# An attention block with a GLU block: VectorE's share of the exponentials as four bit patterns, and projections as column tiles

## The chip, the cores and the metric

The kernel runs on one core of a Trainium2 chip. The metric is device time in microseconds. A profile of one execution stands beside it, with the start and length of the instructions on each engine: TensorE (PE; its weight loads are PEld), VectorE (DVE), ScalarE (ACT), GpSimd (POOL) and SyncE (SP), which issues the DMAs.

## The reference

One transformer layer on 2048 rows of 640 bf16 numbers. There are 32 heads of 20 numbers, so 2048 x 2048 scores for each head.

```python
qkv = (layernorm(x) @ wqkv).reshape(1, 2048, 3, 32, 20)     # q, k, v
scores = einsum("bhqd,bhkd->bhqk", q, k) * 20 ** -0.5
p = softmax(scores, axis=-1)
h = x + einsum("bhqk,bhkd->bhqd", p, v).reshape(1, 2048, 640) @ wo
n = layernorm(h)
out = h + (gelu(n @ w_gate) * (n @ w_up)) @ w_down          # inner width 1728
```

## The kernel before

**Tiles, units and slots.** Scores are computed with the keys on the partitions: a tile is 128 keys by 512 columns in one PSUM bank, made by `qk_mms` (L873) from 32-row tiles of the array, one head in each row group, so that up to four matmuls run at once. The queries are cut into seven chunks, c0 to c6, of 512, 512, 256, 256, 256, 128 and 128 rows (`SIZES`). A chunk is worked through in slots: a slot holds 512 columns of queries and heads (one group of four heads for 512 queries, two groups for 256, four for 128) against all keys, which is always 64 tiles. There are 32 slots (8, 8, 4, 4, 4, 2, 2) and 2048 tiles. A quad is the four tiles of one group of heads and one stretch of keys, one for each head `j`.

ScalarE takes the tiles in units of two or three neighbouring banks, with one `exp` ACTIVATE for each unit (`unit`). In c0 and c4 to c6 the units use banks 0 to 2 and 3 to 4 in turn; in c1 to c3 banks 0 to 2 and 3 to 5 (`PAT`). The results lie in a ring of 18 tiles (`PR` in pts, `PR2` in pts2, which the profile names rege).

**VectorE's exponentials.** Some tiles are left to VectorE (`D_PER_SLOT`: 8 a slot, 2 in the first slot, 6 in c6; 246 in all). `d_exp` reads the scores out of PSUM as 16-bit integers of the exponent scaled by 512 (L831). For each pair of such tiles six operations follow on 1024 columns: two make the mantissa, two square and multiply, one adds, and one turns the sum into the bit pattern of a bf16 number. A VectorE tile's scores go to a spare bank (`BG`), or in c1 to c3 into the third bank of a unit.

**Value matmuls.** Exponentials of a tile are multiplied with 21 columns of `v_all` (20 values and a one, for the softmax's sum) in column tiles of the array, `tile_position=(0, 32 * j)`, so that the four heads of a quad run at once and add up in bank 6 for the whole slot. Two quads go together (`PV_QUADS`). VectorE's tiles are added to quads of ScalarE's that lack a head, at least eight units later (`D_LAG`), and the rest at the slot's end. At the end of a slot `epilogue` copies bank 6 out, transposes it (fp32, L984) and divides by the sums.

**Work around it.** Before the first exponential come layer norm, transposes of x (L576), and the first projections. The other projections of q, k and v run during c0 (`chain`, L631, full 128 x 128 array; evictions on VectorE at L661 and L764). After each chunk `post` makes wo (also `chain`), the second layer norm, gate and up matmuls (`mms`, L1061), GELU on ScalarE in blocks of up to 2048 columns, the product (L1107), the down matmul (L1118) and the output, while the next chunks' exponentials run. What c6 needs, and what c5 left over, comes at the end.

**The order of the work.** The program is a list of operations with reads, writes and PSUM banks. `Sched.schedule` plans it: each engine takes the ready operation of best priority (scores and exp 0, value matmuls 1, projections 1.5 to 3, GLU 3) by costs written into the code, and the planned order is fixed for each engine. Each TensorE operation has a mode: "row" for scores, "col" for value matmuls, "full" for the rest. A change of mode is costed at 0.098 us, and behind an operation of one mode a ready one of the same mode is preferred. `due` is the time by which the next score group must start; an operation that would run past it is passed over. Where TensorE would be idle, the planner adds matmuls that keep its clock up: pads on bank 6 (zero weights, column tiles) and `warm` matmuls on bank 7.

Of the kernel before, what the change touches and what calls it, by code (L numbers as in the profile page):

```python
# [7 lines left out]
ALU = mybir.AluOpType  # L8
# [35 lines left out]
class Sched:  # L44
# [46 lines left out]
    def schedule(self):  # L91
# [23 lines left out]
        while done < total:  # L115
# [4 lines left out]
            for e in ENGINES:  # L120
# [8 lines left out]
                while ready[e]:  # L129
# [203 lines left out]
def bass_sequential_preLN__mha_block__glu_gated_geglu__prompt_kernel(  # L333
# [12 lines left out]
    with ExitStack() as es:  # L346
# [48 lines left out]
        E_WORDS = 19200  # L395
# [39 lines left out]
        dv = [ka[:, 1024 * i:1024 * i + 1024].bitcast(I16) for i in range(ND - 2)]  # L435
        pts2 = carve(PR2 * 512)


        carve = carver(qt_all[:, 0, :, :].rearrange("p g s -> p (g s)"), NG * 512)
        dv += [carve(1024).bitcast(I16) for _ in range(2)]  # L440
        df1 = carve(1024)
        dw1 = carve(1024).bitcast(F16)
        dv0 = [ha_f[:, 1024 * i:1024 * i + 1024].bitcast(I16) for i in range(ND)]
        df0, dw0 = ha_f[:, 1024 * ND:1024 * ND + 1024], ha_f[:, 1024 * ND + 1024:1024 * ND + 2048].bitcast(F16)
# [184 lines left out]
        def chain(bk, key, n, steps, reads, prio, acq=True, after=()):  # L629
            for k, (l, r) in enumerate(steps):  # L630
                yield op("pe", lambda eng, l=l, r=r, k=k: eng.matmul(  # L631
                    bank(bk, n), l, r, start=(k == 0), stop=(k == len(steps) - 1)),
                    c_mm(n), prio, mode="full", util=n / 2400.0, reads=reads, writes=[key], acq=[bk] if (k == 0 and acq) else [],
                    after=after if k == 0 else ())

# [145 lines left out]
        PAT = [((0, 1, 2), (3, 4, 5)) if c in (1,2,3) else ((0, 1, 2), (3, 4)) for c in range(len(CHUNKS))]  # L781
        units, ubank, dtile, ends = [], [], [], []
        i, in_slot = 0, {}
        while i < len(tiles):
            s_ = tiles[i][0]
            c = slots[s_][0]
            bs = PAT[c][len(units) % 2]
            k = in_slot.setdefault(s_, [0, 0])
            nd = D_PER_SLOT[c] if s_ else D_SLOT0
            units.append(tiles[i:i + len(bs)])  # L790
            ubank.append(bs[0])
            six = len(PAT[c][1]) == 3
            i += len(units[-1])
            want = min(nd, (k[0] - D_FIRST) * nd // D_SPAN + 1) if k[0] >= D_FIRST else 0
            if six and k[1] < want and len(units[-1]) == 3 and units[-1][2][0] == s_:
                dtile.append(units[-1].pop())
                k[1] += 1
            elif not six and k[1] < want and tiles[i][0] == s_:
                dtile.append(tiles[i])
                k[1] += 1  # L800
                i += 1
            else:
                dtile.append(None)
            k[0] += 1
            ends.append(i)
        assert all(k[1] % 2 == 0 for k in in_slot.values())
        d_tiles = set(x for x in dtile if x)
        x_unit = {}
        for u, tl in enumerate(units):
            for x in tl + [dtile[u]]:  # L810
                x_unit[x] = u
        pv_bank = {}
        pv_open = set()
        pv_wait = []
        last_qk = {c: [] for c in range(len(CHUNKS))}
        d_raw, d_done = [], []
        d_n = [0]
        d_ops = []
# [3 lines left out]
        def d_exp(b, tile, prio):  # L822

            i, h = (d_n[0] // 2) % ND, d_n[0] % 2
            d_n[0] += 1
            assert all(x[1] != ("dv", i) for x in d_done)
            early = slots[tile[0]][0] == 0
            v = (dv0 if early else dv)[i]
            df, dw = (df0, dw0) if early else (df1, dw1)
            aft = tuple(e_ops) if early else tuple(e_ops) + tuple(last_qk[0])  # L830
            d_ops.append(op("dve", lambda eng: eng.tensor_scalar(v[:, 512 * h:512 * h + 512], bank(b), EXP_MUL, -32000.0,  # L831
                                                                 ALU.mult, ALU.max), c_dve(512), P_QK,
                            reads=[("SD", tile)], writes=[("dv", i)], rel=[b], after=aft))
            d_raw.append(tile)
            if h == 0:
                return
            zi = df.bitcast(I16)
            d = lambda fn, n, r, w: d_ops.append(op("dve", fn, 0.066 + n, prio, reads=r, writes=w))
# [6 lines left out]
            for k, tl in enumerate(d_raw):  # L845
                d_done.append((v[:, 512 * k:512 * k + 512].bitcast(BF16), ("dv", i), tl))
            d_raw.clear()

        def unit(u):
# [56 lines left out]
            while pv_wait:  # L906

                quads = []
                while pv_wait and len(quads) < PV_QUADS:
                    x0 = pv_wait[0][2]  # L910
                    have = [x for x in pv_wait if x[2][:3] == x0[:3]]
                    want = 4 - sum(1 for j in range(4) if x0[:3] + (j,) in d_tiles)
                    if len(have) < want or quads and quads[0][0][2][0] != x0[0]:
                        break
                    del pv_wait[0:want]
                    quads.append(have)
                if not quads:
                    return
                s_ = quads[0][0][2][0]
                c, gs = slots[s_]  # L920
                q0, nq = CHUNKS[c]
                nk = 512 // nq
                final = quads[-1][0][2][1:3] == (gs[-1], NT // nk - 1)
                if len(quads) < PV_QUADS and not final:
                    pv_wait[0:0] = [x for h in quads for x in h]
                    return

                for have in quads:
                    for x in list(d_done):
                        if u - x_unit[x[2]] >= D_LAG and x[2][3] not in [y[2][3] for y in have]:  # L930
                            have.append(x)
                            d_done.remove(x)
                while final and d_done:
                    have = []
# [276 lines left out]
```

## Time and profile before

| what | value |
|---|---|
| runs of the kernel, us | 923.36, 927.22, 928.9 (median 927.22) |
| the profiled execution: span, us | 923.6 |
| ScalarE busy, us (share) | 887.4 (96%), 786 instructions |
| TensorE busy, us (share) | 835.0 (90%), 10070 matmuls |
| VectorE busy, us (share) | 760.3 (82%), 1562 instructions |
| exp ACTIVATEs: of three tiles, of two | 394, 310 |
| first exp starts, last ends, us | 35.3, 891.3 |
| granted TensorE clock, mean | 0.996 |

The profiled execution's own time is known as its span, 923.6 us, which lies at the lower end of the three runs. "Busy" is the time in which at least one instruction of the engine runs. A matmul of 512 columns is shown with 0.38 us, though one can start every 0.217 us; so TensorE's busy share says little of how full it is, and the prediction counts array time instead. Consecutive exps overlap in the same way by about 0.2 us. A group's line in the profile gives: line, engine, operation, out<-in, partitions x elements and type, count | busy us, mean ns of one | idle time of the engine just before them, and what ended it.

### The profile page before, as it was taken

What the parts mean: (1) busy time and instruction counts of PE and PEld (TensorE: products, weight loads), DVE (VectorE), ACT (ScalarE), POOL (GpSimd) and SP (SyncE); (2) the same over time, 40 slices, a digit from 0 to 9 for tenths busy, and PEclk for the clock granted to TensorE, in tenths of its full rate; (3) what the DMA queues carried; (4) which work ended last, traced back from release to release, by engine and by line L of the source; (5) the groups of instructions that cost most, each with busy time, mean ns of one, the idle gap of its engine ahead of it and who ended that gap; (6) DMA issues with size and microseconds to landing.
All of it is one profiled execution on the core that took longest, in us unless ns stands there. A gap on an engine that the chain in (4) does not pass through costs nothing.

```text
span 923.6 us, 23026 instructions
## 1 busy us (share of the span) xinstructions
PE 835.0 (90%) x10070; PEld 353.3 (38%) x10070; DVE 760.3 (82%) x1562; ACT 887.4 (96%) x786; POOL 34.4 (4%) x117
## 2 busy tenths in 40 slices
PE   3999999999998997999788997889999999998998
PEld 2432232222222222233233332334445455565666
DVE  8859999899897896888698995878898769997653
ACT  7899999999999999999999999999999999999981
POOL 5000000000001000000001000000101000001000
PEclk9999999999999999999999999999999999999999
DMA  7301021222721000000111000000100000110000
GB/s 258 95 21 41 17 55 48 71 56 67 228 99 30 1 2 1 1 8 16 37 30 30 2 2 1 2 23 24 44 17 16 1 9 23 26 37 10 10 16 16
DMA packets 39516, 34.36 MB, mean 37 GB/s; under 512 B 19436, under 2 KB 36936, under 8 KB 39416
## 3 DMA queue, kind: packets, MB, share of 16 engines
q1 hardware_dynamic: 39416, 32.89, 12.6%
q8 instruction: 79, 1.29, 0.6%
q14 instruction: 21, 0.17, 0.1%
HBM read 20.12 MB, written 8.09 MB: 31 GB/s over the span
## 4 chain that ended last, share of the span: by engine, by line
ACT 73%; PE 20%; DVE 4%; DMA 2%; SPq 0%; issue 0%
ACT pts L354 46%; ACT rege L354 26%; PE ps L873 5%; PE ps L1061 5%; PE ps L354 4%; PE ps L631 3%; PE ps L1118 3%; DMA regw<-in_A_wqkv_dram 1%; DVE rege L354 1%; ACT L354 1%; DVE rege L831 1%; DVE qt_all L354 1%; PE ps L576 0%; DMA rege<-o_nat 0%; DVE rege L1107 0%; SPq L354 0%
## 5 line engine op out<-in xcount | busy, mean ns | idle before, releaser
L354 ACT ACTIVATE pts<-ps 128x1536 bf16<-128x1536 f32 (+1 forms) x474 | 573.2, 1378 | 5.6 <-PE ps L873 4.5
L873 PE MATMUL ps<-qt_all,kt_all 32*128 32x256 bf16 (+2 forms) x3584 | 289.6, 289 | 48.9 <-ACT pts L354 28.3
L354 ACT ACTIVATE rege<-ps 128x1536 bf16<-128x1536 f32 (+1 forms) x230 | 292.1, 1380 | 2.1 <-PE ps L873 1.1
L873 PEld LDWEIGHTS ps<-qt_all,kt_all 32*128 32x128 bf16 x3584 | 91.3, 92 | 271.5 <-ACT pts L354 155.9
L1061 PE MATMUL ps<-rege,regw 128*128 128x256 bf16 (+2 forms) x980 | 159.2, 292 | 10.5 <-DVE rege L1107 4.8
L354 DVE TENSOR_TENSOR qt_all<-qt_all 128x1024 f16<-128x1024 f16 (+1 forms) x235 | 160.6, 683 | 3.3
L831 DVE TENSOR_SCALAR rege<-ps 128x512 int16<-128x512 f32 x152 | 104.3, 686 | 39.7 <-PE ps L873 38.8
L354 PE MATMUL ps<-pts,v_all 128*21 128x256 bf16 (+2 forms) x2122 | 136.3, 290 | 0.0
L354 PE MATMUL ps<-rege,v_all 128*21 128x256 bf16 (+2 forms) x1278 | 108.2, 292 | 0.0
L1061 PEld LDWEIGHTS ps<-rege,regw 128*128 128x128 bf16 x980 | 73.3, 98 | 70.9 <-issue 24.1
L631 PE MATMUL ps<-regw 128*128 128x512 bf16 (+1 forms) x360 | 87.0, 350 | 2.9 <-DVE v_all L764 1.4
L1118 PE MATMUL ps<-regw,rege 128*128 128x320 bf16 x448 | 78.3, 301 | 2.6 <-DVE rege L1107 1.6
L354 DVE TENSOR_SCALAR qt_all<-qt_all 128x1024 int16<-128x1024 int16 (+1 forms) x188 | 75.9, 420 | 1.5
L831 DVE TENSOR_SCALAR qt_all<-ps 128x512 int16<-128x512 f32 x94 | 64.3, 684 | 3.3 <-PE ps L873 3.0
L354 DVE TENSOR_TENSOR rege<-rege 128x1024 f16<-128x1024 f16 (+4 forms) x103 | 65.4, 644 | 0.8
L354 PEld LDWEIGHTS ps<-pts,v_all 128*21 128x21 bf16 x2122 | 49.2, 91 | 38.2 <-issue 32.6
L354 DVE TENSOR_SCALAR rege<-rege 128x1024 int16<-128x1024 int16 (+2 forms) x136 | 55.4, 424 | 1.2
L354 PE MATMUL ps<-kt_all,zer 128*32 128x512 bf16 x608 | 51.9, 385 | 0.0
L1107 DVE TENSOR_TENSOR rege<-rege,ps 128x512 bf16<-128x512 bf16 (+1 forms) x53 | 35.8, 678 | 19.3 <-PE ps L1061 19.1
L1118 PEld LDWEIGHTS ps<-regw,rege 128*128 128x128 bf16 x448 | 36.9, 98 | 32.2 <-issue 12.4
L354 PEld LDWEIGHTS ps<-rege,v_all 128*21 128x21 bf16 x1278 | 39.2, 91 | 19.8 <-issue 14.5
L631 PEld LDWEIGHTS ps<-regw 128*128 128x128 bf16 x360 | 28.6, 98 | 47.1 <-issue 21.9
(95 smaller groups left out, 579.3 us busy)
## 6 DMA issues: line engine op xcount, KB each, us to landing
rege<-in_A_x_dram SPq DMA_DIRECT2D x6, 640.0 KB, 5.3
q_rows<-regw SPq DMA_DIRECT2D x20, 128.0 KB, 1.7
out_dram<-rege SPq DMA_DIRECT2D x16, 160.0 KB, 1.8
regw<-in_B_w_gate_dram SPq DMA_DIRECT2D x1, 2160.0 KB, 11.5
regw<-in_B_w_up_dram SPq DMA_DIRECT2D x1, 2160.0 KB, 16.5
regw<-in_B_w_down_dram SPq DMA_DIRECT2D x1, 2080.0 KB, 21.6
kt_all<-k_rows SPq DMA_DIRECT2D x12, 160.0 KB
qt_all<-q_rows SPq DMA_DIRECT2D x12, 160.0 KB
```

The source lines that it names most:

```text
L354: return lambda eng: getattr(eng, method)(*args, **kwargs)
L631: yield op("pe", lambda eng, l=l, r=r, k=k: eng.matmul(bank(bk, n), l, r, start=(k == 0), stop=(k == len(steps) - 1)), c_mm(n), prio, mode ...
L831: d_ops.append(op("dve", lambda eng: eng.tensor_scalar(v[:, 512 * h:512 * h + 512], bank(b), EXP_MUL, -32000.0, ALU.mult, ALU.max), c_dve( ...
L873: return lambda eng: eng.matmul(out()[:, kk * nq:(kk + 1) * nq], kt_all[32 * j:32 * j + 32, g, kt * 128:(kt + 1) * 128], qt_all[32 * j:32 ...
L1061: op("pe", lambda eng, a=a, f=f, fi=fi: eng.matmul(bank(bk)[:, fi * nq:(fi + 1) * nq], w[:, a, F0[f]:F0[f] + 128], hnT[:, a, 128 * tb:128 ...
L1107: hdone.append(op("dve", lambda eng, bu=bu, fv=fv, w=w: eng.tensor_tensor(fv, fv, bank(bu, w), ALU.mult), c_dve(w), p, reads=[ku] + hkeys( ...
L1118: op("pe", lambda eng, f=f, o=o, hf=hf, bk=bk: eng.matmul(bank(bk, 320), ha_f[:, o:o + 128], wd[:, f, hf * 320:(hf + 1) * 320], start=(f = ...
```

## The change

It touches four things.

First, VectorE's tiles are whole quads (`D_QUADS`: 3 a slot in c0 to c2, 2 in c3 to c5, 1 in c6, none in the first slot; 79 in all). `d_exp` reads the four tiles out into one buffer of 2048 columns as before. Then four operations, in place of six for each pair, each turn the 16-bit integers into a bf16 bit pattern, `0.25 * v + off`, with four different offsets. The sum of the four numbers, which are piecewise linear in the exponent with their kinks in different places, is the approximation of exp. The sum is never formed: each of the four patterns is multiplied with the values as a quad of its own (`pv_op`), and PSUM adds them.

Second, `chain`, `mms` and the down matmul no longer use the full array: `col4` issues each as four matmuls with 32 weight columns in the four column tiles, in mode "col".

Third, the pattern of units is three and two tiles in all chunks (`SIX` is empty); VectorE's tiles always get a spare bank (7 or 5). The ring of results is 16 tiles (`PR2` 4). A slot's value matmuls are kept in order of slots: terms of a later slot wait in `d_wait` until the slot before is closed, and the last group of a slot waits for all groups of it.

Fourth, the planner adds an event at the time `due` where it passes an operation over.

```diff
                     if e == "pe" and due is not None and o.prio[0] > 0 and t < due < t + o.dur + (MODE_SWITCH[e] if mode[e] not in (None, o.mode) else 0):
                         skipped.append((p, i))
+                        if due not in events:
+                            heapq.heappush(events, due)
...
-CA, CB, CC = -0.277383, 1.25604202, 1.0 - 11.0 / 128
+TERM_LOG = 1233.0 / 512
+TERMS = tuple(128.0 * (127.0 - TERM_LOG) + o / 4.0 + 0.125 for o in (0, 90, 211, 365))
+NTERM = len(TERMS)
 PV_QUADS = 2
-D_LAG = 8
-PR, PR2 = 12, 6
-ND = 4
-D_PER_SLOT = (8,8,8,8,8,8,6)
-D_SLOT0 = 2
-D_FIRST, D_SPAN = 1, 16
+PR, PR2 = 12, 4
+D_QUADS = (3, 3, 3, 2, 2, 2, 1)
+D_QUADS0 = 0
+SIX = ()
+D_FIRST, D_SPAN = 0, 18
...
+        d_v = [d_early[0:2], d_late[0:2], d_late[0:2]]
+        d_a = [d_early[2:3] + d_any, d_late[2:3] + d_any, d_late[2:3] + d_any + d_last]
...
             for k, (l, r) in enumerate(steps):
-                yield op("pe", lambda eng, l=l, r=r, k=k: eng.matmul(
-                    bank(bk, n), l, r, start=(k == 0), stop=(k == len(steps) - 1)),
-                    c_mm(n), prio, mode="full", util=n / 2400.0, ...
+                yield op("pe", col4(lambda bk=bk: bank(bk, n), l, r, k == 0, k == len(steps) - 1),
+                    c_mm(n), prio, mode="col", util=n / 2400.0, ...
+
+        def col4(out, l, r, start, stop):
+            return [lambda eng, j=j: eng.matmul(out()[32 * j:32 * j + 32], l[:, 32 * j:32 * j + 32], r, start=start, stop=stop,
+                                                tile_position=(0, 32 * j), skip_group_check=True) for j in range(4)]
...
-        PAT = [((0, 1, 2), (3, 4, 5)) if c in (1,2,3) else ((0, 1, 2), (3, 4)) for c in range(len(CHUNKS))]
+        PAT = [((0, 1, 2), (3, 4, 5)) if c in SIX else ((0, 1, 2), (3, 4)) for c in range(len(CHUNKS))]
+            want = min(nd, (k[0] - D_FIRST) * nd // D_SPAN + 1) if k[0] >= D_FIRST and nd else 0
...
             d_raw.append(tile)
-            if h == 0:
+            if h < 3:
                 return
-            d(I("tensor_scalar", zi, v, 511, 2048, ALU.bitwise_and, ALU.bitwise_or), 0.265, [("dv", i)], ["df"])
-            d(I("tensor_scalar", dw, zi, CA / OCT, CB, ALU.mult, ALU.add), 0.265, ["df"], ["dw"])
-            d(I("tensor_tensor", dw, dw, dw, ALU.mult), 0.53, ["dw"], ["dw"])
-            d(I("tensor_tensor", dw, dw, zi, ALU.mult), 0.53, ["df", "dw"], ["dw"])
-            d(I("tensor_tensor", v, v, dw, ALU.add), 0.53, ["dw", ("dv", i)], [("dv", i)])
-            d(I("tensor_scalar", v, v, 0.25, 16256.0 + 128.0 * (CC - 1.0), ALU.mult, ALU.add), 0.265, [("dv", i)], [("dv", i)])
+            d_n[e] += 1
+            for off in TERMS:
+                a, ak = d_a[e][d_t[e] % len(d_a[e])]
+                d_t[e] += 1
+                d_ops.append(op("dve", I("tensor_scalar", a, v, 0.25, off, ALU.mult, ALU.add), 0.686, prio,
+                                reads=[vk], writes=[ak], after=aft))
+                pv_op([[(a[:, 512 * k:512 * k + 512].bitcast(BF16), ak, x) for k, x in enumerate(d_raw)]], tile[0])
+            d_raw.clear()
+
+        def pv_op(quads, s_):
+            if s_ != pv_slot[0]:
+                d_wait.append((quads, s_))
+                return
...
+            last = pv_n[0] == len(gs) * NT // nk + (NTERM - 1) * len(d_kb[s_])
+            if first:
+                pv_ops.append(Bank(6))
+            i = op("pe", fns, 0.218 * len(quads), P_PV, mode="col", util=0.213 * len(quads), reads=reads,
+                   writes=[("O", s_)] if last else [("Oq", s_, pv_n[0])], acq=pv_ops[0:1] if first else [],
+                   after=pv_ops[1:] if last else pv_ops[1:2])
+            pv_ops.append(i)
+            if last:
+                sc.final.add(i)
+                epilogue(s_, pv_ops[0])
```

The gate and up matmuls (`mms`) and the down matmul are changed in the same way as `chain`.

More of the change, by code (lines that the diff above doesn't have):

```diff
@@ L394, in bass_sequential_preLN__mha_block__glu_gated_geglu__prompt_kernel @@
         W_WORDS = NA * DFF * 2 + NF * D
-        E_WORDS = 19200
+        E_WORDS = 19712
         regw = sb("regw", [128, W_WORDS])
@@ L822, in d_exp @@
         def d_exp(b, tile, prio):
[L824 to L830, printed above, removed]
+            c = slots[tile[0]][0]
+            e = min(c, 2)
+            h = len(d_raw)
+            v, vk = d_v[e][d_n[e] % len(d_v[e])]
@@ new lines, in unit @@
+            while len(pv_wait) >= 4:
+                s_ = pv_wait[0][2][0]
+                n = len([x for x in pv_wait if x[2][0] == s_]) // 4
+                left = sum(1 for v in range(u + 1, len(units)) for x in units[v] if x[2 - 2] == s_)
+                if n < PV_QUADS and left:
+                    return
+                quads = [pv_wait[4 * k:4 * k + 4] for k in range(min(n, PV_QUADS))]
+                del pv_wait[0:4 * len(quads)]
+                assert all(len({x[2][:3] for x in h}) == 1 for h in quads)
+                pv_op(quads, s_)
```

176 lines of the change are left out of this document (72 added, 104 removed).

## The prediction

> **What bounds the kernel now.** I read the page first (sections 1 and 4), then the groups by shape, the chain of waits in order of time, busy time by stage, and the timeline of single groups. The page says which engine is never free:
>
> ```profile
> PE 835.0 (90%) x10070; PEld 353.3 (38%) x10070; DVE 760.3 (82%) x1562; ACT 887.4 (96%) x786; POOL 34.4 (4%) x117
> ...
> ACT 73%; PE 20%; DVE 4%; DMA 2%; SPq 0%; issue 0%
> ```
>
> ScalarE is busy 96% of the span and carries 73% of the chain that ended last. The groups by shape say with what:
>
> ```profile
> L354 ACT ACTIVATE pts<-ps 128x1536 bf16<-128x1536 f32 x263 | 400.6, 1569 | 5.5 <-PE ps L873 4.5 <-PE ps L354 0.7
> L354 ACT ACTIVATE pts<-ps 128x1024 bf16<-128x1024 f32 x211 | 240.4, 1139 | 0.1
> ...
> L354 ACT ACTIVATE rege<-ps 128x1536 bf16<-128x1536 f32 x131 | 201.1, 1569 | 1.8 <-PE ps L873 1.1 <-PE ps L354 0.5
> ...
> L354 ACT ACTIVATE rege<-ps 128x1024 bf16<-128x1024 f32 x99 | 111.9, 1131 | 0.4 <-PE ps L354 0.4
> ```
>
> 394 exps of three tiles and 310 of two: 1802 of the 2048 score tiles; the other 246 are VectorE's. The means, 1569 and about 1136 ns, differ by 0.432 us, the price of one tile. They overlap, so what an exp really takes is read from the chain in order of time, in a stretch where threes and twos alternate:
>
> ```profile
> 145.17 4.52 ACT pts L354 x4
> 151.95 4.52 ACT pts L354 x4
> 158.73 4.52 ACT pts L354 x4
> 165.51 4.52 ACT pts L354 x4
> ```
>
> Each row starts 6.78 us after the last, with six exps in between (four into pts, two into rege): 2.26 us for a three and a two, so 1.346 and 0.914, which is 0.432 a tile and 0.05 an instruction. All exps: 394 x 1.346 + 310 x 0.914 = 814 us. They run from 35.3 to 891.3, 856 us; about 37 us of this is GELU with its table loads in five places. So ScalarE waits hardly at all (856 - 814 - 37 = 5 us): what shortens its list shortens the span, unless something else then comes late.
>
> The next engine is TensorE. Its busy 90% counts latency, so I counted array time: columns streamed, at the spacing of matmuls in the timeline.
>
> ```profile
> 165.94 0.39 PE L873 MATMUL ps<-qt_all,kt_all 32*128 32x512 bf16 x2
> ...
> 166.26 1.04 PE L631 MATMUL ps<-regw 128*128 128x512 bf16 x4
> ...
> 892.04 0.63 PE L354 MATMUL ps<-pts,v_all 128*21 128x128 bf16 x32
> ...
> 908.27 7.99 PE L1061 MATMUL ps<-rege,regw 128*128 128x128 bf16 x140 [0.39 <-ACT rege L582]
> ```
>
> Full-array matmuls of 512 columns start (1.04 - 0.39) / 3 = 0.217 us apart, of 128 columns (7.99 - 0.22) / 139 = 0.056. Value matmuls in column tiles run four at once: 32 of 128 columns are eight groups, (0.63 - 0.22) / 7 = 0.058 each; groups of 512 columns stand 0.2195 apart in long runs. Where the tile shape changes, as from the score group at 165.94 to the projection at 166.26, 0.32 passes where 0.217 would do: a switch costs 0.10. I counted 1545 switches between 35 and 891 us (150 us), 175 of them between column tiles and the full array.
>
> By chunk of queries (length; array work without filler matmuls, plus switches, as a share of it): c0 206.7, 84%; c1 212.7, 75%; c2 110.1, 71%; c3 101.7, 81%; c4 114.0, 88%; c5 51.4, 90%; c6 59.4, 88%. Filler (pads and clock-keeping matmuls, 53 us) runs where there is nothing else. Against the shortest spacing of exps (1.335 and 0.905 us), slots without GELU lose 0.36 us on average, those of c4 and c5 up to 0.96. VectorE by stage, c0, c1 and c5:
>
> ```profile
> 35.30:242.00 206.70, 197.19 (x1593) 60.01 (x1593) 178.19 (x363) 205.93 (x183) 0.62 (x1) 1.00 0.19 54
> 242.00:454.70 212.70, 189.63 (x1563) 59.21 (x1561) 177.28 (x345) 211.80 (x179) 4.61 (x14) 1.00 0.13 41
> ...
> 780.50:832.00 51.50, 49.91 (x1178) 31.39 (x1176) 46.93 (x99) 51.00 (x47) 2.61 (x14) 1.00 0.15 29
> ```
>
> The fifth figure of a row is VectorE's busy time: 86%, 83%, 91%. It is no bound, but not idle.
>
> **The change part by part.**
>
> *ScalarE's list.* VectorE takes quads of four tiles: none in slot 0, then 7 x 3 + 8 x 3 + 4 x 3 + 4 x 2 + 4 x 2 + 2 x 2 + 2 x 1 = 79, that is 316 tiles. ScalarE keeps 1732: -70 tiles. With threes and twos alternating everywhere these are 693 exps, 11 fewer. Gain 70 x 0.432 + 11 x 0.05 = **-30.8 us**: c0 -11.8, c1 -14.0, c2 -7.0, c3 to c5 +0.2, c6 +1.8 (4 tiles more). GELU is untouched. This lies on the bound all along.
>
> *VectorE's work.* A pair of tiles now costs two evictions at 0.686 and six operations (3 x 0.42 and 3 x 0.68): 4.68 us; 123 pairs, 575 us. A quad costs four evictions and four 2048-wide operations:
>
> ```profile
> L354 DVE TENSOR_SCALAR rege<-rege 128x2048 int16<-128x2048 int16 x2 | 1.4, 694 | 0.1
> ...
> L831 DVE TENSOR_SCALAR rege<-ps 128x512 int16<-128x512 f32 x58 | 39.7, 685 | 4.4 <-PE ps L873 4.1
> ```
>
> (c0 alone.) The 2048-wide row is the same kind in 16 bits, so a quad is 4 x 0.686 + 4 x 0.69 = 5.5 us; 79 take 435 us. VectorE loses 140 us of work for 30.8 us of span. Worth 0 in itself.
>
> *Value matmuls.* Now 131 us without filler: 2048 tiles would need 512 groups, 112 us, and the rest goes on groups that VectorE's tiles leave incomplete. After: 433 groups from ScalarE's tiles and 79 x 4 from the terms, all of four: 749 x 0.2195 = 164. TensorE +34 us: c0 +7, c1 +12, c2 +5, c3 +4, c4 +3, c5 +2, c6 +1.
>
> *Score matmuls of VectorE's tiles.* In c1 to c3 they rode in the third bank of a unit; now each is a group of its own. In c0 such groups add 0.09 us each; 176 of them, less fewer units: c1 +6, c2 +3, c3 +3.
>
> *Column-tile projections and GLU matmuls.* 1948 matmuls become four each. The nearest rows are the value groups: 0.058 for 0.056 at 128 columns, 0.2195 for 0.217 at 512, so +0.0025 to +0.004 each, 6 us over the kernel. Against that, the 175 switches between column tiles and the full array mostly go, and some 25 visits fall away with the units: -19 us. What stays full (transposes) now pays a switch beside projections: head and tail have few, +0.4 and +0.6 with the slower matmuls there, both on the path. From both sides: the value groups load 4 x 21 weight columns within 0.058; 4 x 32 have no row at 128 columns. If loading is free, 0; if it limits the value groups, 128/84 x 0.058 = 0.088 a group, +0.032 over today's 0.056, on 280 of them +9 us, 4.4 of it in the tail. I take the low end: the 128-column loads of the full array keep up with 0.056.
>
> The Trainium skill's "TensorEngine Tiling (Array Packing)", section "Gotcha 2: Feature Incompatibilities", speaks against this part: column tiling and Fast Weight Load exclude each other. By it the full-array 0.056 would not carry over and the sum would go towards the +9; no run here loads 32-column tiles at such a pace.
>
> *TensorE in sum.* Need over window after: c0 175 of 195 (90%), c1 174 of 199 (88%), c2 82%, c3 87%, c4 90%, c5 94%, c6 87%. Only c5 is above what the kernel already bears (90%). The 20 slots of c0 to c2 come to the load of today's c4 and c5, so I take 0.2 us more waiting each, **+4 us**, and +0.5 in c5. Bounds: 0 (waits stay) and 20 x 0.96 = +19.
>
> *Buffers and waits.* ScalarE's ring of exp results falls from 18 tiles to 16; with threes and twos alternating a place still comes back after six units (once in a long while five). VectorE's term operation now waits until TensorE has read its buffer (two buffers, three from c2); queued behind it are evictions that free score and projection banks. TensorE is then at most 2 us from that group, and VectorE has 10 to 20% free, so 0.
>
> *The planner's extra event* lets TensorE look for work again when a score group falls due; it can only fill gaps: 0, at most -0.36 x 32 = -11.
>
> **Sum.** 923.6 - 30.8 + 4.5 + 0.4 + 0.6 = 898.3 us of span. The profiled span stands 3.6 us below the median of the runs (927.2): **902 us**.
>
> **Rivals.**
> *A, weight loading limits column tiles* (the skill's rule above, as a mechanism): the tail's 140 GLU groups go from 8.0 to 12.4 us, c6 gets slower too. For: nothing shows 32-column loads at this pace. Against: 0.056 in the full array. 902 + 4.4 to 9 = 906 to 911. Chance 0.12.
> *B, TensorE becomes the bound*: each slot of c0 to c2 and c5 loses 1 us more, 22 us: 924. For: 94% in c5, 90% in c0, where projections have due times. Against: c4's and c5's small waits today, and the filler that gives way. Chance 0.15.
> *C, slower: the slot's close.* All value matmuls of a slot share bank 6, which the next slot gets only after the last term. A slot's last VectorE tile comes with unit 17 of about 21; then eviction 0.69, four terms 2.8, a group 0.22, copy 0.69: 4.4 us, when 4.3 us of exps remain. The ring holds six units, 6.8 us, so ScalarE stops once the close slips by about 6 us. With 31 such slots, 1 us of stop in each costs the whole 30.8; 1.5 us gives 902 + 46 = 948. For: VectorE is 83 to 91% busy, and the order is fixed beforehand. Against: 6 us of slack, and VectorE is relieved. Chance 0.13.
>
> **How the numbers follow.** My forecast has 0.60. One per cent, 9 us, is about what a measurement of this kernel can tell from no change: below 918 is faster, above 936.5 slower. Faster: 0.60 + 0.12 + 0.05 of B = 0.77; within: the rest of B and a mild C, 0.11; slower: 0.12. The range runs from 892 (waits shrink through the planner's event) to 925 (B) and leaves out C.
>
> **What would show it.** Right: 693 exps at 2.26 us a pair, the last one ending near 865 us; 316 evictions at 0.686 and 316 terms at 0.69; about 749 value groups; far fewer switches; less filler; the tail still 32 to 33 us. Wrong: GLU groups of 128 columns above 0.06 (A); ScalarE idle over 1 us a slot behind score matmuls, with TensorE's gaps closed (B) or at slot ends behind bank 6 (C).

## The result, and the profile after

The changed kernel takes 932.0 us (median of four runs, 931.05 to 932.97); the kernel before, beside it on the same chip, 926.1 us (923.36 to 928.9). The ratio is 1.0069, with a 95% interval of 1.0043 to 1.0095: 0.7% slower, within the 1% that the prediction calls no change. The forecast was 902 us, with 892 to 925 as its range. The profiled execution has a span of 930.6 us (before 923.6; forecast for the span 898.3).

First the page of the changed kernel: the busy time of the engines, the queue that brings instructions, and the chain that ended last.

```profile
PE 857.2 (92%) x16754; PEld 390.6 (42%) x16754; DVE 650.6 (70%) x1210; ACT 863.2 (93%) x775; POOL 31.8 (3%) x117
...
q8 instruction: 131, 2.15, 1.0%
...
ACT 52%; PE 39%; DVE 5%; DMA 2%; issue 2%; DVEq 0%
```

ScalarE lost 24 us of busy time and VectorE 110, as the change means it to. But ScalarE now carries 52% of the chain where it had 73%, TensorE 39% where it had 20%, and "issue" (waiting for nothing that the profile shows) has gone from 0 to 2%. The instruction queue brings 2.15 MB in 131 packets; before, 1.29 MB in 79.

The groups by shape show the lists of ScalarE and VectorE:

```profile
L357 ACT ACTIVATE pts<-ps 128x1024 bf16<-128x1024 f32 x347 | 372.9, 1075 | 1.0 <-PE ps L914 0.5 <-PE ps L357 0.2
L357 ACT ACTIVATE pts<-ps 128x1536 bf16<-128x1536 f32 x231 | 345.9, 1497 | 19.3 <-PE ps L914 17.7 <-PE ps L357 0.4
L357 ACT ACTIVATE rege<-ps 128x1536 bf16<-128x1536 f32 x115 | 172.4, 1499 | 7.2 <-PE ps L914 6.8
...
L835 DVE TENSOR_SCALAR rege<-ps 128x512 int16<-128x512 f32 x200 | 137.2, 688 | 77.7 <-PE ps L914 75.2
L357 DVE TENSOR_SCALAR rege<-rege 128x2048 int16<-128x2048 int16 x132 | 89.0, 686 | 2.2 <-PE ps L357 1.1
```

347 + 231 + 115 = 693 exps, as forecast, but the exps of three tiles now stood idle for 26.5 us, 24.5 of it behind score matmuls (L914); before, the same rows had 5.5 + 1.8. Where nothing is late, the pace is the forecast's, as the chain in order of time shows:

```profile
174.40 1.34 ACT rege L357
175.74 5.44 ACT pts L357 x5
181.18 1.45 ACT rege L357
```

Six exps in 6.78 us, 2.26 for a three and a two. So the list got shorter as forecast and the waits ate it. Busy time by stage cuts the span at the first exp's start and the last exp's end (the columns: window, length, then busy us and instructions of PE, PEld, DVE, ACT and POOL, granted clock, DMA share, GB/s):

```profile
39.40:889.10 849.70, 801.86 (x15070) 351.30 (x15073) 604.81 (x1079) 827.38 (x717) 19.61 (x85) 0.99 0.13 33
889.10:930.60 41.50, 30.78 (x1292) 24.66 (x1280) 13.40 (x32) 11.02 (x14) 0.00 (x0) 0.96 0.06 20
```

| us | before | forecast | after | missed by |
|---|---|---|---|---|
| first exp starts | 35.3 | 35.7 | 39.4 | +3.8 |
| first exp to the last one's end | 856.1 | 829.8 | 849.7 | +19.9 |
| from there to the end | 32.2 | 32.8 | 41.5 | +8.7 |
| span | 923.6 | 898.3 | 930.6 | +32.3 |

The middle row can be taken apart. From the start of one exp to the start of the next, beyond the shortest spacing of its kind (1.335 us behind a three and 0.905 behind a two), ScalarE lost 13.6 us before, outside GELU, and loses 37.7 now: +24.1, where the forecast had +4.5. Stops are counted in this way below; a stop's idle time in a view is 0.1 to 0.4 us less. Of the 37.7 us, 10.7 lie at 329 to 333 us (slot 11) and 6.3 at 144 to 153 us (from the end of slot 3); the other slots lose 0.7 us on average (before 0.4).

Two places stand out. **The stop at 319 us** (slot 11, in c1), from the timeline of ScalarE, TensorE and SyncE:

```profile
308.05 0.53 SPq L357 DMA_DIRECT2D regw<-in_B_w_down_dram  x1
308.62 13.94 SPq L357 DMA_TRANSPOSE rege<-xn_t  x1
...
319.10 1.34 ACT L357 ACTIVATE pts<-ps 128x1024 bf16<-128x1024 f32 x1
328.10 1.05 PE L637 MATMUL ps<-rege,regw 128*32 128x512 bf16 x8 [9.00 <-DMA rege<-xn_t]
329.73 2.54 ACT L357 ACTIVATE pts<-ps 128x1536 bf16<-128x1536 f32 x2 [9.30 <-PE ps L914]
```

A transpose of c0's normed rows is issued on SyncE's queue behind the 6.4 MB of GLU weights and lands 19.4 us later; the three before it took 2.6 to 2.7 us each. TensorE, whose order is fixed, stands at the gate matmul that needs it for 9.0 us; the next score group is queued behind that matmul; ScalarE stops for 9.3 us (9.7 by the spacing of exps). In the kernel before, the weights were issued at 239 to 240 us, long before the transposes. They must wait for the last projection, because they take over its buffers, and this one now starts at 291.0 us instead of 230.6. That goes with the quads: without them (e2, below) it ends at 214.6. It is not the added value matmuls themselves, since it still ends at 296.4 with 237 value groups fewer (e9). What in the quads moves it is not shown.

**The end**, TensorE's timeline of the last chunk's own gate and up matmuls:

```profile
910.96 1.97 PE L637 MATMUL ps<-rege,regw 128*32 128x128 bf16 x128 [0.17 <-issue]
914.99 3.16 PE L637 MATMUL ps<-rege,regw 128*32 128x128 bf16 x128 [2.06 <-issue]
918.75 2.04 PE L637 MATMUL ps<-rege,regw 128*32 128x128 bf16 x128 [0.59 <-issue]
922.22 1.01 PE L637 MATMUL ps<-rege,regw 128*32 128x128 bf16 x58 [1.43 <-issue]
```

The 140 groups that took 8.0 us before take 14.3 (from 908.95, where the first 118 matmuls start). Within a burst at full clock nothing is slow: by the sum that the prediction used, (1.97 - 0.22) / 31 = 0.056 us a group, as in the full array. (The burst of 3.16 us ran while the granted clock was half, from 915.5 to 918.9.) Between bursts TensorE waits for no semaphore. The three full bursts are of 128 matmuls, and 128 matmuls with their 128 loads are one packet of the instruction queue: 2.15 MB for twice 16754 instructions are 64 bytes each, 256 in 16 KB. The packets start at 908.7, 912.6, 916.2, 919.8 and 923.3 us, and each burst begins 2.2 to 2.6 us after one. So the reading to test was that the instructions themselves arrive too slowly.

### The profile page after: what moved, and what is told of

Read it like the earlier page. It is cut to its first block, busy times and chain, and to the rows that moved or that the text cites. A ratio compares the mean times of both kernels' runs of the same rounds, so it can differ in the third digit from the quotient of the medians.

```text
span 930.6 us, 35945 instructions
## 1 busy us (share of the span) xinstructions
PE 857.2 (92%) x16754; PEld 390.6 (42%) x16754; DVE 650.6 (70%) x1210; ACT 863.2 (93%) x775; POOL 31.8 (3%) x117
## 3 DMA queue, kind: packets, MB, share of 16 engines
q8 instruction: 131, 2.15, 1.0%
## 4 chain that ended last, share of the span: by engine, by line
ACT 52%; PE 39%; DVE 5%; DMA 2%; issue 2%; DVEq 0%
ACT pts L357 40%; PE ps L637 19%; ACT rege L357 11%; PE ps L914 11%; PE ps L357 8%; DMA rege<-xn_t 2%; DVE rege L835 1%; DVE stats L357 1%; PE ps L979 1%; DVE rege L357 1%; ACT L357 1%; PE ps L577 0%; DVE kt_all L357 0%; DVE rege L1101 0%; DVE rege L1024 0%
## 5 line engine op out<-in xcount | busy, mean ns | idle before, releaser
L357 ACT ACTIVATE pts<-ps 128x1536 bf16<-128x1536 f32 x578 | 652.8, 1244 | 20.2 <-PE ps L914 18.3
L914 PE MATMUL ps<-qt_all,kt_all 32*128 32x256 bf16 (+2 forms) x3584 | 325.9, 289 | 24.1 <-ACT pts L357 16.8
L914 PEld LDWEIGHTS ps<-qt_all,kt_all 32*128 32x128 bf16 x3584 | 104.1, 92 | 248.8 <-ACT pts L357 137.3
L637 PE MATMUL ps<-rege,regw 128*32 128x256 bf16 (+2 forms) x3920 | 167.1, 295 | 21.5 <-DMA rege<-xn_t 9.0
L357 ACT ACTIVATE rege<-ps 128x1536 bf16<-128x1536 f32 x115 | 172.4, 1499 | 7.2 <-PE ps L914 6.8
L357 PE MATMUL ps<-rege,v_all 128*21 128x512 bf16 (+2 forms) x1564 | 130.0, 313 | 1.1 <-DVE rege L357 1.1
L637 PEld LDWEIGHTS ps<-rege,regw 128*32 128x32 bf16 x3920 | 82.8, 98 | 69.4 <-issue 29.7
L637 PE MATMUL ps<-regw 128*32 128x512 bf16 (+1 forms) x1440 | 91.7, 357 | 2.2 <-DVE v_all L768 0.6
L357 DVE TENSOR_SCALAR rege<-rege 128x2048 int16<-128x2048 int16 x132 | 89.0, 686 | 2.2 <-PE ps L357 1.1
L637 PE MATMUL ps<-regw,rege 128*32 128x320 bf16 x1792 | 84.9, 301 | 1.5 <-DVE rege L1080 0.6
L357 PE MATMUL ps<-qt_all,v_all 128*21 128x256 bf16 (+2 forms) x1048 | 54.5, 282 | 0.6 <-DVE qt_all L357 0.4
L637 PEld LDWEIGHTS ps<-regw,rege 128*32 128x32 bf16 x1792 | 42.3, 96 | 26.1 <-issue 13.6
L1090 DVE CAST rege<-ps 128x512 bf16<-128x512 f32 (+1 forms) x53 | 36.2, 682 | 21.4 <-PE ps L637 21.1
L357 DVE TENSOR_SCALAR qt_all<-rege 128x2048 int16<-128x2048 int16 x70 | 47.3, 686 | 1.0 <-PE ps L357 0.4
```

The source lines that it names most:

```text
L357: return lambda eng: getattr(eng, method)(*args, **kwargs)
L637: return [lambda eng, j=j: eng.matmul(out()[32 * j:32 * j + 32], l[:, 32 * j:32 * j + 32], r, start=start, stop=stop, tile_position=(0, 32 ...
L914: return lambda eng: eng.matmul(out()[:, kk * nq:(kk + 1) * nq], kt_all[32 * j:32 * j + 32, g, kt * 128:(kt + 1) * 128], qt_all[32 * j:32 ...
L1090: cp.append(op("dve", lambda eng, bg=bg, fv=fv, w=w: eng.tensor_copy(fv, bank(bg, w)), c_dve(w), p, reads=[kg], writes=hkeys(k), rel=[bg], ...
```

## The experiments

Theories at the start. *W* (the prediction's rival A): 32-column weight loads are slow. *S*: instruction supply; a packet comes every 3.4 us at best, and four matmuls with four loads for each group of 128 columns use one up in 2 us. *L*: the late weights make the stop of slot 11. *T*: TensorE, which the prediction let bear 34 us of added value matmuls, has no room for them.

**One half of the change each.** e1: the quads, with projections, gate, up and down as full-array matmuls (`col4` given the width 128). e2: the kernel before, with the column tiles alone.

```diff
-                                                tile_position=(0, 32 * j), ...) for j in range(4)]
+            if w == 128:
+                return [lambda eng: eng.matmul(out(), l, r, start=start, stop=stop)]
```

> The four-pattern quads alone: projections, gate, up and down matmuls on the full array again, all else as in the changed kernel. Theory S (TensorE's instructions are supplied too slowly once each matmul is four, and the new mode moves projections ahead of what the first exp needs): the first exp starts at 35 to 36 us instead of 39.4, the end part after the last exp takes 32 to 33 us instead of 41.5, the kernel comes to about 915 us or less. Rival B (the added value matmuls fill TensorE): it stays at 930 or above, since these remain and switches of shape come back.

Measured: 915.5 us, ratio 0.9885 (0.9854 to 0.9915). First exp at 35.9, last one's end 873.3, end part 40.0.

> The column tiles alone: the kernel before, with projections, gate, up and down matmuls as four column-tile matmuls each. Theory S: first exp at about 39 us, end part 40 to 42 us, so about 926 + 4 + 9 = 939 us, less what fewer switches give back. Rival B: no added value matmuls, fewer switches, so 926 or below.

Measured: 942.3 us, ratio 1.0192 (1.0155 to 1.023). First exp at 38.5, end part 41.7, own gate and up matmuls 13.6 us. So the quads gain about 11 us and the column tiles cost about 18; the sum, +7, is close to the +6 of the whole change. But the quads' gain is a third of the 30.8 forecast, and their end part did not return to 32.

**W against S.** e3: the changed kernel, with gate and up matmuls of 128 rows in two tiles of 64 columns, half the instructions.

```diff
-  hnT[:, a, 128 * tb:128 * tb + nq], a == 0, a == NA - 1),
+  hnT[:, a, 128 * tb:128 * tb + nq], a == 0, a == NA - 1, 64 if nq == 128 else 32),
```

> The changed kernel, but the gate and up matmuls of the two 128-row chunks as two column tiles of 64 weight columns instead of four of 32: half the instructions at the same array time. Theory S: 560 gate and up matmuls of the last chunk become 280, the end part falls from 41.5 to about 35 us, the kernel to about 925. Rival W (it is the loading of weights in column tiles that is slow, not the number of instructions): the same columns are loaded by fewer loads, the end part stays at 40 to 42 us and the kernel at 932.

Measured: 922.8 us, ratio 0.9977 (0.996 to 0.9994), 9 us less than the changed kernel; end part 29.3. The same 140 groups in its timeline:

```profile
905.33 8.21 PE L639 MATMUL ps<-rege,regw 128*64 128x128 bf16 x280 [0.97 <-ACT rege L583]
```

One run of 280 matmuls without a gap. Both forms are column tiles and load the same columns; what has been halved is the number of instructions: S.

**Is it the order?** The planner orders column tiles otherwise than full-array work. e5: the kernel before with its own planned order, every matmul only issued as four; e6: the same, with two tiles for 128 rows.

```diff
-  bank(bk, n), l, r, start=(k == 0), stop=(k == len(steps) - 1)), c_mm(n), prio, mode="full",
+  col4(lambda bk=bk: bank(bk, n), l, r, k == 0, k == len(steps) - 1), c_mm(n), prio, mode="full",
```

> The kernel before in its own planned order (the planner still sees the mode of the full array), each projection, gate, up and down matmul issued as four column-tile matmuls. This parts the two costs seen in the run of the column tiles alone (942 us): the supply of instructions and the order that the new mode leads to. Theory S: first exp back at 35.3 to 35.8 us, end part 38 to 39 us (only the 14.4 us instead of 8.0 for the last gate and up matmuls remains), so 931 to 934 us. Rival (order alone): 926 or below.

> As the run before, but the gate and up matmuls of the 128-row chunks as two column tiles of 64 columns, so half the instructions there. Theory S: end part 32 to 33 us again and 925 to 928 us, though these are still column tiles. Rival W (column tiles load weights slowly): as the run before.

Measured: e5 941.3 us, 1.0181 (1.0148 to 1.0213), more than expected; e6 926.5, 1.0021 (1.0006 to 1.0035). In e5 the first exp starts at 38.8, the stretch of exps takes 856.2 us, the same as before, and the end part 47.1 (10.4 us of it "issue" in front of matmuls of 128 columns, and 6.8 us at half clock). So the order isn't the cause of the 18 us, and where ScalarE is the bound the column tiles cost nothing: all of it lies ahead of the first exp and behind the last. The end of e5 shows the supply in its purest form:

```profile
920.99 1.97 PE L636 MATMUL ps<-rege,regw 128*32 128x128 bf16 x128 [2.29 <-issue]
924.74 1.97 PE L636 MATMUL ps<-rege,regw 128*32 128x128 bf16 x128 [1.78 <-issue]
928.49 1.97 PE L636 MATMUL ps<-rege,regw 128*32 128x128 bf16 x128 [1.78 <-issue]
932.24 0.74 PE L636 MATMUL ps<-rege,regw 128*32 128x128 bf16 x40 [1.78 <-issue]
```

Bursts of 128 matmuls start exactly 3.75 us apart. e6, with half the instructions, ends with an end part of 31.4.

**The late weights.** e4: the weight loads are issued after c0's transposes. (The expectation calls theory L "Theory S on the stop".)

```diff
+                if c == 0:
+                    for i in wld:
+                        sc.ops[i].deps.update(sc.lw[("hnT", tt)] for tt in range(4))
```

> The changed kernel, but the loads of the GLU weights are issued only after the four DMA transposes of c0's second layer norm have landed. Theory S on the stop of 9.7 us in slot 11 (the fourth transpose queues behind 6.4 MB of weights, and TensorE's next gate matmul waits for it in front of the score matmuls): the stop and the half-speed clock after it go, about 932 - 10 = 921 to 924 us. Rival: the GLU matmuls of c0 come later by the load's 20 us and the loss returns elsewhere, 930 to 934.

Measured: 924.2 us, ratio 0.9983 (0.9963 to 1.0003). The 9.7 us stop of slot 11 is gone; stops of 1.8 and 0.8 remain there. Theory L holds, and 8 of the 10 us come back.

> The changed kernel with two of its losses taken out together: two column tiles of 64 in the 128-row chunks, and the weight loads after the DMA transposes of c0. If the two are independent, 932 - 9 - 8 = 915 us; if what is saved in front comes back as GLU work left for the end, 920 or above.

e7 (e3 and e4 together): 913.2 us, 0.9874 (0.9849 to 0.9898). The two causes add up: 19 us.

**Two smaller suspects and other mixtures.** e10 takes out the planner's added event (the last two lines of the first block of the change). e8 has full-array matmuls in the head and for gate and up matmuls up to 256 rows, and e11 full-array matmuls for gate and up up to 256 rows; both with the late loads.

> The changed kernel without the planner's extra event. Every theory: no difference that can be measured, 930 to 934 us; the prediction costed the event at 0 with up to 11 us of gain.

> The best version that the experiments point to: the four-pattern quads, column tiles only where a group has 320 columns or more and after the first scores, full array for the projections before the first exp and for gate and up matmuls of 256 and 128 columns, weight loads after c0's DMA transposes. Theory S: first exp near 36 to 37.5, no stop of 9 us in slot 11, end part 33 to 40 (work left over), 905 to 915 us, below both kernels. Rival B: about 925, since the value matmuls remain.

> The changed kernel with late weight loads, and gate and up matmuls of 256 and 128 columns on the full array (512 columns, projections, wo and down stay column tiles). Against the run with two tiles of 64 in the 128-row chunks (913 us) it takes the load off the instruction supply in c2 to c4 too, and pays switches. Theory S, if supply also costs in c2 to c4: below 913 us; if supply only costs at 128 columns: 913 to 918.

Measured: e10 930.9, 1.0053 (1.0035 to 1.007): no difference to the changed kernel, as the prediction's 0. e8 916.9, 0.99 (0.9861 to 0.9938). e11 914.2, 0.9867 (0.9845 to 0.989). e8 misses its 905 to 915, and its first exp starts at 39.4 instead of 36 to 37.5. e11 is in the second of its cases: full-array matmuls of 256 columns bring nothing more. Neither beats e7: the last exp ends earlier (e11: 873.5 us, e7: 879.6) or the stops are other ones (e8: 5.8 us, ending at 149), and the end part is 40.1 (e8) and 37.3 us (e11). This pattern, also e1's, was the open point: when the exps end early, the end part grows.

**How much do the value matmuls of the added patterns cost?** e9: e1 with the first of the four patterns multiplied only (and the count of groups that closes a slot lowered to match).

```diff
+                if off == TERMS[0]:
-                pv_op([[(a[:, 512 * k:512 * k + 512].bitcast(BF16), ak, x) ...
+                    pv_op([[(a[:, 512 * k:512 * k + 512].bitcast(BF16), ak, x) ...
```

> The quads with the full array (915 us), but only the first of the four patterns goes into value matmuls; VectorE still computes all four. Left out: 237 groups of value matmuls, so the softmax weights of these tiles are too small. It measures what the added groups cost. Theory B as a part of the truth (they crowd GLU work out to the end, 40 us there, and stop ScalarE in c0): the end part falls to about 32 us, the stops in c0 shrink, about 898 to 902 us, where the prediction stood. Rival: they are hidden, as predicted up to 4 us, and it stays at 910 to 915.

Measured: 930.3 us, 1.0041 (1.0016 to 1.0066): a miss by some 30 us. The row of the granted clock, in the profiled execution of 936.4 us, tells a part of why:

```profile
PEclk9999977999979979999999999999999999889999
```

Its mean is 0.947; before the last exp there are thirteen stretches at half clock, of 3.4 to 17 us each, 96 us in all (e1: 14 us). With less work on TensorE the clock had fallen. That led to something the prediction had overlooked: the kernel before lays pads (short zero matmuls that keep the clock) behind value operations, 33 us of them (608 matmuls, four at once), and the planner knows a value operation by its tag `"O"`. The change tags all but a slot's last `"Oq"`. So the changed kernel has no pads at all. Four more runs give them back (e13: the changed kernel, e14: the fastest version, below; e15: one pattern, e16: all four, both on the full array).

```diff
-                if e == "pe" and self.pad is not None and o.tag and o.tag[0] == "O":
+                if e == "pe" and self.pad is not None and o.tag and o.tag[0] in ("O", "Oq"):
```

> The changed kernel, with the clock-keeping copies of short matmuls again allowed behind every value operation of a slot, not behind the last alone (as the kernel before has them). P (the missing copies cost clock, and so part of the 25 us that ScalarE's waits rose): half-clock stretches behind the stops of slots 3 and 11 go, granted clock 0.99 or more, 5 to 10 us faster than the changed kernel's 932: 922 to 927. Q (TensorE is short of room, so copies only take it from needed work): no gain, 930 to 937. The slot 11 wait for the late weights stays in both.

> The quads on the full array with the value matmuls of the first of the four patterns alone (237 value groups of the other three patterns are left out), as in the run that fell to half clock, but with the copies of short matmuls again allowed behind every value operation. If the half clock of that run came from the missing copies, the clock returns to 0.985 or more and the time falls from 930 to 900-912; the difference to the quads with all four patterns and the same copies is then what the added value groups cost. If the clock stays near 0.95, the copies aren't what keeps it, and the time stays at 925 or more.

> All four patterns on the full array (the quads alone, 915.5) with the copies of short matmuls again allowed behind every value operation: the partner of the run with one pattern. P: 3 to 8 us faster, 908 to 912. Q: same or slower, 914 to 920. The run with one pattern is faster than this one by the price of the 237 added value groups: 0 to 3 us if they fill idle room of TensorE, as the prediction had it for most chunks, 8 to 15 us if TensorE is short of room where they stand.

Measured: e13 929.9 us, 1.0036 (1.0014 to 1.0058), clock 0.994: hardly any gain, so Q holds for the time. Its stages are the most telling rows of the study:

```profile
38.60:869.10 830.50, 800.39 (x14901) 345.90 (x14911) 597.88 (x1067) 819.65 (x714) 19.43 (x85) 0.99 0.13 33
869.10:928.40 59.30, 44.98 (x1942) 38.20 (x1942) 20.68 (x44) 14.20 (x16) 0.00 (x0) 1.00 0.05 15
```

The stretch of exps takes 830.5 us, the forecast's 829.8 to within 1 us, but by luck. In the order that the planner makes with pads, the transposes of c0 come ahead of the weights, so that slot 11 has no stop (10.7 us of the gain), and one of the five GELU blocks of the stretch (6 us) has moved behind the last exp. The end part is 59.3 instead of 41.5, with 1942 matmuls in it instead of 1292: the GLU work that found no room before the last exp is done after it. What the stretch gained, 19 us, came back as 18 us of a longer end part.

e16: 938.4 us, 1.014 (1.011 to 1.017), clock 0.98; slower than either theory had it. e15: 921.3 us, 0.994 (0.9909 to 0.9971), clock 0.976, between its two cases. Their stages, e16 first:

```profile
35.40:885.40 850.00, 804.49 (x10559) 323.88 (x10622) 596.18 (x1062) 821.06 (x713) 17.49 (x76) 0.98 0.12 31
885.40:939.60 54.20, 50.04 (x570) 41.54 (x567) 24.87 (x52) 14.31 (x17) 1.72 (x10) 1.00 0.07 23
```

```profile
34.90:892.80 857.90, 795.05 (x9567) 326.23 (x9620) 613.53 (x1090) 828.97 (x721) 19.64 (x85) 0.98 0.12 32
892.80:922.00 29.20, 21.64 (x238) 16.79 (x237) 9.07 (x24) 6.64 (x11) 0.00 (x0) 0.94 0.04 12
```

237 value groups (52 us of array time) fewer: the end part falls from 54.2 to 29.2 us, with 332 matmuls fewer in it. The pair without pads says the same of the end part (e1 40.0, e9 28.9). In the total time the pairs disagree: with pads four patterns cost 17 us more than one, without pads 15 us less. These totals hold two things besides the value groups. One is the clock: in e9 the exps lose 35 us within the half-clock stretches (the stop shown next among them), in e1 3 us. The other is the stop of the late weights. e1 has escaped it, since its order issues all four transposes ahead of the weights; e9, e15 and e16 have it. TensorE's rows in e9 and in e16:

```profile
336.78 1.03 PE L638 MATMUL ps<-rege,regw 128*128 128x512 bf16 x2 [9.73 <-DMA rege<-xn_t]
```

```profile
348.91 1.03 PE L638 MATMUL ps<-rege,regw 128*128 128x512 bf16 x2 [7.89 <-DMA rege<-xn_t]
```

ScalarE stops for 10.4 us there in e9, 8.5 in e16 and 12.0 in e15. Of the 21 us between the profiled executions of e1 and e9 (913.3 and 934.4), 9 are that stop, 18 are other waits, mostly at half clock, 5 a GELU block more in the stretch, and the end part takes off 11.

So that the added groups push other work past the last exp is shown by both pairs; what they cost in time by themselves is not settled. The same stop is most of why pads seem to cost 23 us on the full array (e16 against e1) and nothing in column tiles (e13 against the changed kernel): the end part grows in both, by 14 and 18 us, but the order with pads brings the late stop to e16 (7 us more there than in e1) and takes it away from e13 (10.7 us less).

**The fastest version.** e12: e7, with `D_FIRST` 1 in place of 0 (the quads start one step later in a slot) and two quads in c6's slots in place of one. e14: the same with pads.

> The version with two tiles of 64 and late loads (913 us), with quads begun one unit later in a slot and two quads instead of one in the slots of c6, so that the order has no stop in the last slot (4.4 us before). If that stop was a real loss: about 909 us; if its time was work for TensorE that now comes at the end: 912 to 915.

> The fastest version so far (909.95: late weight loads, two-tile gate and up matmuls for chunks of 128 rows, one more quad in the last chunk, quads from a slot's second tile) with the copies of short matmuls again allowed behind every value operation. P: 4 to 8 us faster, 902 to 906. Q: same or slower, 909 to 915.

Measured: e12 909.95 us, 0.982 (0.9801 to 0.984), the fastest of all; e14 910.6, 0.9832 (0.9804 to 0.9859), no gain from the pads here either. e12 comes where its first case had it, but hardly for that reason: the 4.4 us break in e7's last slot is a GELU block on ScalarE, and in e12 it has moved behind the last exp, where the end part grows by 5.3 us. The gain of 3.3 us is about what eight tiles fewer on ScalarE are worth by the prediction's price (8 x 0.432); as two things were changed at once, this is not shown.

## Why the prediction was wrong

**Right.** The gain on ScalarE's list: 693 exps at 2.26 us a pair. VectorE's prices: 316 evictions at 0.688 and terms at 0.686. The value groups: 749. The planner's event: nothing (e10). Rival C's absence: of ScalarE's idle time among the exps only 0.6 us is put down to value matmuls, and most slots lose under 1 us. The low end of the price of loading: groups of four 32-column loads start 0.056 us apart inside a burst, as in the full array, so rival A's mechanism is not there. Its sign, groups above 0.06, would have been misread without the gaps: 14.3 us for 140 groups are 0.10 each.

**Wrong: "Column-tile projections and GLU matmuls ... I take the low end."** Both ends of that bound were about loading. The count of instructions, which the change multiplies by four, had no term. The profile before had the row: 79 packets of 16 KB, never less than 4.0 us apart; in the changed kernel they are never less than 3.4. It showed the queue, but not its limit. By e5's bursts a packet, 128 loads and 128 matmuls, lasts 3.75 us: 14.6 ns an instruction, so 0.117 us for a group of eight where the array needs 0.056. By an estimate from these numbers, groups of 256 columns (0.108 us, half of 0.217) lie at the limit too, though e11 shows no loss there. The tail term, +0.6, measured +9.3, 6.3 of it in the 140 groups shown, of which about 1 goes with the half clock (e3, with half the instructions in these groups, has an end part 12 us shorter, 4 of them a GELU block that moved ahead of the last exp). The Trainium skill's "Runtime: NRT & Kernel Launch", section "Instruction fetch mechanics", says that instructions come in blocks of 16 KiB and that crossing to the next is mostly hidden. The size agrees with the 131 packets of 2.15 MB. For short matmuls the crossing isn't hidden here: TensorE stands for 1.78 us at each block of e5's end.

**Wrong: "head ... +0.4".** It measured +4.2. In all variants with column-tile projections the first exp starts at 38.1 to 40.6 us (e5 and e6, in the order of before, 38.8 and 38.4), with full-array ones at 34.9 to 36.2 in e1, e9, e15 and e16, but at 39.4 in e8. A part is the clock: projections of 512 columns start 0.427 us apart until it is granted in full and 0.216 after that, which came at 18.8 us before and at 21.2 after. In e7, where it came at 18.7, the first exp starts at 38.1; in e11, at 23.1, it starts at 40.6. So about 1.3 of the 4.2 us go with the later clock, and some 3 with the form of issue. Changes of tile shape are a small part of these: the head has 8 where it had 1, 0.7 us at the prediction's 0.10. The rest is open.

**Wrong: "Buffers and waits ... 0".** I looked at rings and banks, not at what a later end of the projections moves on SyncE's queue. With the quads the last projection came 60 us later, the weights with it, and a transpose landed behind 6.4 MB: 8 us (e4).

**Wrong: "TensorE in sum ... +4 us".** The need was sized well: by the prediction's counting 88% of the stretch of exps is array time and switches (before 80%, forecast 82 to 94 by chunk), though switches fell by 72, not by about 200 (the 175 between column tiles and the full array fell to 50, and others came). What failed is the step from the load to the waits: ScalarE's waits rose by 24 us, not by 4.5, and not as 0.2 us in every slot. Seventeen of the 37.7 us lie in two places, the late transpose and a stop of 4.4 us behind a run of 76 projection matmuls, with 1.9 us soon after it (e3, e4, e7, e10 and e11 show the 4.4 us too; why the planned order puts the run there is not shown). And work is left for after the last exp (e1, e8, e11, e13, e16: end parts of 37 to 59 us, where the prediction let it all be done in time). Rival B named the right engine, and its 22 us of waits are near the measured rise, but by luck: it looked for 1 us in every slot, and almost half of the rise is the late transpose, which is no lack of room on TensorE.

**Wrong: the filler "runs where there is nothing else".** It vanished through a tag, not because TensorE was full. In the changed kernel that cost little in time (e13: 2 us, within the interval's reach); on a less loaded TensorE it costs clock (e9 0.947, e15 with pads 0.976) and 9 us (930.3 against 921.3).

In sum, of the 30 us missed, e3 and e4 give back 9 and 8 by themselves and 19 together (e7). e7's profiled execution is still 12.9 us above the forecast of the span (911.2 and 898.3): 2.4 in the head, 7 in waits beyond the forecast, the stop of 4.4 us in slot 3 among them, and 4.3 for a GELU block that now stands ahead of the last exp, less 1.2 in the end part. For the work left behind the last exp, TensorE's lack of room is the explanation that e13 and the pairs of e1 with e9 and e16 with e15 support, by their end parts; for the stop in slot 3 it is argued, not shown.

## What to carry to other kernels

When a change multiplies the number of instructions, price their supply as a resource of its own: look at the spacing of the instruction packets and at "issue" gaps between bursts of equal count, before thinking of the array. When the bound engine's list gets shorter by giving work to the next one, ask where that one's background work will finish: here, with some 90% of TensorE's time needed in most stages, part of the gain reappeared behind the last piece of the bound engine. And follow what a pushed-back stage releases late (here a buffer, the loads into it, and a small transfer queued behind them). When two variants are compared, look first whether both have the same stops: a new order can add one or take one away that has nothing to do with what was changed.

## What the runs showed of the hardware that was not expected

In none of these kernels did two 16 KB packets of the instruction queue start less than 3.34 us apart, and in e5's steady run TensorE was fed one every 3.75 us. Two tiles of 64 columns did 140 groups of 128 columns in 8.0 to 8.2 us, as fast as the full array (8.0), so loads into column tiles weren't slower here; at four instructions for 0.057 us this form stands right at the 14.6 ns an instruction of e5's supply. And with work taken off TensorE the clock fell: with 237 groups fewer and no pads the mean granted clock went from 0.993 (e1) to 0.947 (e9), in half-clock stretches that are multiples of 3.4 us. Pads alone, with the same groups, brought it back to 0.976 and took 9 us off the time (e15).
